# A two-layer mixture of experts in split fp32: first layers of nine units by seven block products

## The chip, the cores and the metric

The kernel runs on one core of one Trainium2 chip. TensorE (PE) does the matmuls, VectorE (DVE), ScalarE (ACT) and GpSimd (POOL) the elementwise work, SyncE (SP) issues most transfers. The metric is device microseconds of one execution; less is better. Three runs of a kernel give a median.

## The reference

```python
# attention: 2 batches x 8 heads, 576 tokens, head size 64; scores under (row maximum - tau) are masked
x = attention(q, k, v, tau)                       # -> x [1152, 512]
for e in range(4):                                # four experts, features 1024
    h = np.maximum(x @ w1[e], 0.0)
    out += p[:, e:e + 1] * (h @ w2[e])
x = out
h = np.maximum(x @ w_in, 0.0)                     # features 2048
return (h * h @ w_out).astype(np.float32)
```

## The kernel before

Every fp32 operand of the experts is split into a high part that TensorE's fast fp32 form holds exactly and a low part, and each product is three matmuls: high x high, high x low, low x high. The last two matrices (w_in, w_out) are taken as two more "experts", so that there are NE = 6, each in two halves of 512 features: twelve **units** (e, half).

A unit has a first layer (`unit_range`, L755): for each of four feature blocks f and each token range, four 128-deep steps of x with three matmuls each, into a "ph" bank. Then ACT writes the ReLU's high part (L764) and DVE its low part (L768); for the last two experts the chain is ACT ReLU (L781), DVE square (L784), ACT high (L787), POOL low (L791), through three "u" buffers. The second layer (`chunk`, L824) is nine token chunks of 128, each twelve 512-wide matmuls into one of two "m" banks, added up on DVE (L836, L840). Three units ("early") take tokens 0 to 511 while attention still runs, and tokens 512 to 1151 after it. The other nine take token ranges of 512, 320 and 320 at once: 48 matmuls of 512 and 96 of 320 in a first layer. In the text "the nine units" are these.

Weights come in groups of 128 x 1024 (`group`): SP loads one into one of two "wraw" buffers, ACT casts the high part (L685), POOL subtracts the low part (L688) into one of four "w" slots; four groups a unit. The weights of the last two experts are stored as 64-bit numbers; `convert` narrows them in 32 steps (L632 load, DVE L637, L642, L647, ACT square L652, DVE L656, L661 store). In the second layer of unit (3, 1), `turn_x` transposes the result into the x of the last two experts (L859, L864, L867).

All operations are put in an order ahead of time: `plan` schedules them by estimated times, ranks (lower goes first) and free slots, PE's own order of units being a fixed chain. Each engine then runs its list in that order, and a waiting instruction holds up what stands behind it on its engine.

Of the kernel before, what the change touches and what calls it, by code (L numbers as in the profile page):

```python
# [18 lines left out]
N = B * S  # L19
# [159 lines left out]
def attention_moe_kernel(ctx, tc, qT, kT, kD, vp, tau, probs, wa, wb, wc, wd, out):  # L179
# [16 lines left out]
        "wraw": 2, "w": 4, "ha": 1, "h": 1, "ph": 4, "wide": 1, "dbl": 2, "u": 3,  # L196
# [411 lines left out]

    def end_attention():
        attn.close()  # L610
        open_pools(ctx, "h", "wide", "dbl", "u")
        rest = ctx.enter_context(tc.tile_pool(name="acc", bufs=1))
        accs[1] = rest.tile([P, NCH - EARLY // P, DM], F32, name="acc1")
        open_pools(ctx, "ph", space=PSUM)
# [8 lines left out]
    def convert(e, w, g):  # L623
        key = e, w, g
        stores[key] = []
        for z in range(2):
            wb_, db = Buf("wide"), Buf("dbl")
# [12 lines left out]
            def second(wb_=wb_, db=db):  # L640
                o = db.tile
# [3 lines left out]
            def third(wb_=wb_, db=db):  # L645
                o = db.tile
                nc.vector.scalar_tensor_tensor(  # L647
                    o, wb_.tile[:, :, 1], -(1 << 30), o, ALU.bitwise_and, ALU.bitwise_or)
# [5 lines left out]
            def fourth(wb_=wb_, db=db):  # L654
                m, f = wb_.tile.bitcast(F32)[:, :, 1], db.tile.bitcast(F32)
                nc.vector.scalar_tensor_tensor(f, m, LEAST, f, ALU.is_ge, ALU.mult)  # L656

            def store(db=db, z=z):
                if key not in narrow:
                    narrow[key] = dram_p.tile([P, 2, 512], F32, tag=f"n{e}{w}{g}", name=f"n{e}{w}{g}")  # L660
                nc.sync.dma_start(narrow[key][:, z], db.tile.bitcast(F32))  # L661
# [34 lines left out]

    pe_last = [None]
# [23 lines left out]

    def unit(e, half, ranges, early):

        rank = 10000 + seq[0]
        gs = [group(e, 0, 2 * half + x, rank) for x in range(2)]
        gs2 = []
        for n0, widths in ranges:
            unit_range(e, half, n0, widths, early, gs, gs2, rank)

    def unit_range(e, half, n0, widths, early, gs, gs2, rank):  # L730
        n1 = n0 + sum(widths)
        firsts = [(n0 + sum(widths[:n]), w) for n, w in enumerate(widths)]

        hb = Buf("ha" if early else "h")
        width = EARLY if early else N
        h_ops = {}

        def h_tiles():
            if hb.tile is None:
                hb.tile = [new(hb, [P, FH, width], F32R, f"{hb.pool}{n}") for n in ("hi", "lo")]  # L740
            return hb.tile

        for f in range(FH):
            for t0, step in firsts:
# [14 lines left out]
                if unturned:  # L759
                    turn_x(unturned.pop())  # L760
                c0 = t0

                def relu(f=f, c0=c0, step=step, pb=pb):
                    nc.scalar.activation(h_tiles()[0][:, f, c0:c0 + step], pb.tile, AF.Relu)  # L764

                def low(f=f, c0=c0, step=step, pb=pb):
                    oh, ol = (h[:, f, c0:c0 + step] for h in h_tiles())
                    nc.vector.scalar_tensor_tensor(ol, pb.tile, 0.0, oh.bitcast(F32), ALU.max, ALU.subtract)  # L768

                r = -5000  # L770
                deps = [last] if early else [last, late]
                if e < E:
                    a = op("ACT", 0.02 + step / 1110, relu, deps, [pb, hb], r, 0.16)
                    b = op("DVE", 0.07 + step / 966, low, [a], [pb, hb], r, 0.15)
                    h_ops[f, t0] = b
                else:
                    ub = Buf("u")

                    def relu_u(ub=ub, pb=pb, step=step):
                        ub.tile = new(ub, [P, step], F32)  # L780
                        nc.scalar.activation(ub.tile, pb.tile, AF.Relu)  # L781

                    def square(ub=ub, pb=pb):
                        nc.vector.scalar_tensor_tensor(ub.tile, pb.tile, 0.0, ub.tile, ALU.max, ALU.mult)  # L784

                    def high2(ub=ub, f=f, c0=c0, step=step):
                        nc.scalar.copy(h_tiles()[0][:, f, c0:c0 + step], ub.tile)  # L787

                    def low2(ub=ub, f=f, c0=c0, step=step):
                        oh, ol = (h[:, f, c0:c0 + step] for h in h_tiles())  # L790
                        nc.gpsimd.tensor_sub(ol, ub.tile, oh.bitcast(F32))  # L791

                    a = op("ACT", 0.12 + step / 1000, relu_u, deps, [pb, ub], r)
                    b = op("DVE", 0.16 + step / 960, square, [a], [pb, ub], r)
                    c = op("ACT", 0.15 + step / 1000, high2, [b], [ub, hb], r + 1)
                    h_ops[f, t0] = op("POOL", 0.2 + 2.6 * step / 1000, low2, [c], [ub, hb], r + 1)
        if not gs2:
            gs2 += [group(e, 1, 2 * half + x, rank + 20) for x in range(2)]
        turned = []
        for n in range(n0 // P, n1 // P):  # L800
            needs = [o for (f, t0), o in h_ops.items() if t0 < (n + 1) * P and n * P < t0 + dict(firsts)[t0]]
# [3 lines left out]
            for cut in cuts:  # L805
                chunk(e, half, n, cut, needs, h_ops, hb, gs2)
            if (e, half) == (E - 1, 1):
                turned.append(n)
                if len(turned) > 1:
                    turn_x(turned[-2])  # L810
        unturned.extend(turned[-1:])

    def chunk(e, half, n, cut, needs, h_ops, hb, gs2):
        ob = Buf("m")
        width = cut.stop - cut.start
        for x in range(2):
            def mm(x=x, n=n, ob=ob):
                if x == 0:
                    ob.tile = new(ob, [P, width], F32)
                for f in (2 * x, 2 * x + 1):  # L820
                    hi, lo = (w[:, f % 2, cut] for w in gs2[x][2].tile)
                    ah, al = (h[:, f, n * P:(n + 1) * P] for h in hb.tile)
# [4 lines left out]
            need = [h_ops[k] for k in h_ops if h_ops[k] in needs and k[0] // 2 == x]  # L827
            last = pe(6 * (width / 2400 + 0.0135), mm, need + list(gs2[x][:2]), [ob, hb, gs2[x][2]])
# [24 lines left out]
    def turn_x(n):  # L853
# [7 lines left out]
        oh, ol = xhi[:, :, n * P:(n + 1) * P], xlo[:, :, n * P:(n + 1) * P]  # L861

# [5 lines left out]

        a = pe(0.45, turn, [acc_ops[n], late], [tb])
        b = op("ACT", 0.6, high, [a], [tb], -4000)  # L870
        x2[n] = op("DVE", 0.7, low, [b], [tb], -4000)

    for e, w, g in NARROWED:
        convert(e, w, g)
    for e, half, ranges, early in UNITS:
# [68 lines left out]
```

## Time and profile before

| | us |
|---|---|
| median of 3 runs (lowest, highest) | 751.4 (750.18, 752.2) |
| span of the profiled execution | 748.9 |
| first and second layer of a full unit | 25.02, 24.50 |

The page has no time of its own for the profiled execution beside its span, which runs from its first to its last instruction; the median of the runs is 2.5 us above it. Matmuls overlap, so a matmul's busy time is longer than the step from one to the next.

### The profile page before, as it was taken

The numbers are of one execution on the slowest core, as the hardware profiler recorded it, in microseconds if no ns is written. First come the engines' busy times: TensorE is split into PE (matmuls) and PEld (weight loads), VectorE is DVE, ScalarE is ACT, GpSimd is POOL, SyncE is SP. The second block draws the span as 40 slices with busy tenths as digits, with TensorE's granted clock in tenths as the row PEclk, the third lists the DMA queues.
The fourth block names the chain that finished last, engine by engine and source line by source line (L and its number), as shares of the span: only waits on it lengthen the run. The fifth ranks groups of instructions, "written<-read, shape, count | busy, mean of one in ns | idle before, by whom it ended". The sixth has DMA issues, their size and how long they took to land.

```text
span 748.9 us, 10557 instructions
## 1 busy us (share of the span) xinstructions
PE 736.9 (98%) x4118; PEld 617.9 (83%) x4118; DVE 376.0 (50%) x692; ACT 307.8 (41%) x542; POOL 325.5 (43%) x284
## 2 busy tenths in 40 slices
PE   7899999999999999999999999999999999999998
PEld 4556677887798998988989889888888898898887
DVE  6877765656256445645447454545665022222222
ACT  5887785756432232312304223123264352250430
POOL 3797879998443333112204121122066173461530
PEclk9999999999999999999999999999999999999999
DMA  6644323111223543433333424332334020100002
GB/s 228 229 145 151 104 59 124 64 56 53 80 83 114 197 145 105 158 112 104 108 112 100 141 72 140 100 112 77 105 106 134 15 84 29 57 29 28 1 29 98
DMA packets 26001, 74.70 MB, mean 100 GB/s; under 512 B 3040, under 2 KB 5472, under 8 KB 25952
## 3 DMA queue, kind: packets, MB, share of 16 engines
q1 hardware_dynamic: 24368, 71.55, 28.9%
q10 hardware_dynamic: 1584, 2.49, 0.9%
q8 instruction: 32, 0.52, 0.3%
q14 instruction: 17, 0.14, 0.1%
HBM read 63.28 MB, written 10.75 MB: 99 GB/s over the span
## 4 chain that ended last, share of the span: by engine, by line
PE 92%; POOL 3%; DVE 2%; ACT 1%; issue 1%; DMA 1%; SPq 0%; DVEq 0%; POOLq 0%; ACTq 0%
PE m L824 39%; PE ph L755 36%; PE tv L543 5%; PE m L755 4%; PE tv L487 4%; PE s L381 2%; PE s L395 2%; DVE nm L400 1%; POOL p L466 1%; DVE p L421 1%; DMA k<-in_kT_dram 1%; POOL wlo L688 1%; PE ph L859 1%; PE tv L508 0%; POOL q L274 0%
## 5 line engine op out<-in xcount | busy, mean ns | idle before, releaser
L688 POOL TENSOR_TENSOR wlo<-wraw,whi 128x1024 fp32r<-128x1024 f32 x60 | 146.9, 2460 | 321.6 <-ACT whi L685 302.0
L755 PE MATMUL ph<-xlo,whi 128*128 128x320 f32 (+1 forms) x528 | 175.0, 331 | 0.0
L755 PE MATMUL ph<-xhi,whi 128*128 128x320 f32 (+1 forms) x528 | 174.9, 331 | 0.0
L755 PE MATMUL ph<-xhi,wlo 128*128 128x320 f32 (+1 forms) x528 | 174.7, 331 | 0.0
L824 PE MATMUL m<-whi,hhi 128*128 128x512 f32 (+1 forms) x388 | 150.9, 389 | 0.0
L824 PE MATMUL m<-wlo,hhi 128*128 128x512 f32 (+1 forms) x388 | 150.2, 387 | 0.0
L824 PE MATMUL m<-whi,hlo 128*128 128x512 f32 (+1 forms) x388 | 150.2, 387 | 0.0
L755 PEld LDWEIGHTS ph<-xhi,whi 128*128 128x128 f32 x528 | 99.1, 188 | 6.4
L755 PEld LDWEIGHTS ph<-xlo,whi 128*128 128x128 f32 x528 | 99.1, 188 | 6.1
L755 PEld LDWEIGHTS ph<-xhi,wlo 128*128 128x128 f32 x528 | 99.1, 188 | 5.9
L685 ACT CAST whi<-wraw 128x1024 fp32r<-128x1024 f32 x60 | 63.2, 1053 | 97.2 <-PE m L824 86.8
L836 DVE SCALAR_TENSOR_TENSOR acc<-m,pn,acc 128x512 f32<-128x512 f32 x63 | 47.3, 750 | 86.6 <-PE m L824 86.6
L824 PEld LDWEIGHTS m<-whi,hlo 128*128 128x128 f32 x388 | 72.9, 188 | 14.9
L824 PEld LDWEIGHTS m<-whi,hhi 128*128 128x128 f32 x388 | 72.9, 188 | 14.4
L824 PEld LDWEIGHTS m<-wlo,hhi 128*128 128x128 f32 x388 | 72.9, 188 | 14.2
L764 ACT ACTIVATE hhi<-ph 128x320 fp32r<-128x320 f32 (+1 forms) x84 | 39.7, 476 | 98.0 <-PE ph L755 97.8
L466 POOL TENSOR_TENSOR p<-p,r 128x576 f32<-128x576 f32 x64 | 72.3, 1149 | 8.8 <-DVE r L448 8.1
L768 DVE SCALAR_TENSOR_TENSOR hlo<-ph,hhi 128x320 fp32r<-128x320 f32 (+1 forms) x84 | 44.7, 537 | 58.0 <-ACT hhi L764 57.8
L784 DVE SCALAR_TENSOR_TENSOR u<-ph,u 128x320 f32<-128x320 f32 (+1 forms) x48 | 26.8, 559 | 83.6 <-ACT u L781 83.5
L791 POOL TENSOR_TENSOR hlo<-u,hhi 128x320 fp32r<-128x320 f32 (+1 forms) x48 | 50.2, 1047 | 31.8 <-ACT hhi L787 30.6
L421 DVE SCALAR_TENSOR_TENSOR p<-s,th,p 128x576 f32<-128x576 f32 x59 | 47.5, 815 | 21.8 <-POOL th L405 15.5
L400 DVE TENSOR_REDUCE nm<-s 128x1 f32<-128x576 f32 x67 | 48.6, 751 | 13.5 <-PE s L381 7.5
(90 smaller groups left out, 911.1 us busy)
## 6 DMA issues: line engine op xcount, KB each, us to landing
wraw<-in_wa_dram SPq DMA_DIRECT2D x22, 512.0 KB, 4.0
wraw<-in_wb_dram SPq DMA_DIRECT2D x22, 512.0 KB, 3.5
wide<-in_wc_dram SPq DMA_DIRECT2D x16, 512.0 KB, 4.4
n<-dbl SPq DMA_DIRECT2D x32, 256.0 KB, 3.4
wide<-in_wd_dram SPq DMA_DIRECT2D x16, 512.0 KB, 3.9
wraw<-n SPq DMA_DIRECT2D x16, 512.0 KB, 3.3
v<-in_vp_dram SPq DMA_DIRECT2D x12, 320.0 KB, 3.2
k<-in_kT_dram SPq DMA_DIRECT2D x8, 432.0 KB, 4.4
```

The costliest lines, as they stand in the source:

```text
L400: nc.vector.tensor_reduce(t["nm"], sb.tile[:, :, :HW], AX.XY, ALU.max, negate=True)
L421: nc.vector.scalar_tensor_tensor(p, sb.tile[:, :, :HW], t["th"], p, ALU.is_ge, ALU.mult, accum_out=sm["sm"][:, z:z + 1])
L466: nc.gpsimd.tensor_mul(p, p, sums[i]["r"][:, y:y + 1].to_broadcast([P, S]))
L543: nc.tensor.matmul(ob.tile[z * D:(z + 1) * D, :], tiles["v"][:, vc, :], pts[g].tile[:, ch, :], start=(n == 0), stop=(n == QT),)
L685: nc.scalar.copy(sb.tile[0], rb.tile)
L688: nc.gpsimd.tensor_sub(sb.tile[1], rb.tile, sb.tile[0].bitcast(F32))
L755: nc.tensor.matmul(pb.tile, w, m, start=(c == 0 and n == 0), stop=(c == DC - 1 and n == 2))
L764: nc.scalar.activation(h_tiles()[0][:, f, c0:c0 + step], pb.tile, AF.Relu)
L768: nc.vector.scalar_tensor_tensor(ol, pb.tile, 0.0, oh.bitcast(F32), ALU.max, ALU.subtract)
L791: nc.gpsimd.tensor_sub(ol, ub.tile, oh.bitcast(F32))
L824: nc.tensor.matmul(ob.tile, w, m, start=(f == 0 and y == 0), stop=(f == FH - 1 and y == 2))
L836: nc.vector.scalar_tensor_tensor(a, ob.tile, pn[:, n, e:e + 1], a, ALU.mult, ALU.add)
```

## The change

The nine units that take all tokens at once get another first layer (`paired`). Weights, x and result are each cut into 2 x 2 blocks: model features in two halves, unit features in two halves, tokens in pairs of 64-token runs (the even runs and the odd runs of each token range). The product of the blocks is taken by seven block products instead of eight. This needs sums of blocks: S1 to S4 of the weights (`sums`, POOL, then split again by ACT and POOL into "s12" and "s34"; A22 is split apart into "a22"), and four sums of x (`th`, `tl`), made once after attention (`pair_up`) and again in `turn_x`. Tokens 0 to 511 and 512 to 1151 are the two groups g; a set is a group and one of two feature blocks, and its products have 256 or 320 columns. Products are accumulated in PSUM banks A, B, C; partial sums that are needed twice are copied by ACT into "sn" (`keep`) and added by DVE (`join`), for one result into a fourth bank D. Products 1 to 3 read x itself, every second run of 64 tokens; 4 to 7 read the sums. "ph" has five banks instead of four. `convert` keeps its unfinished words in a new "pd" bank of PSUM instead of in "dbl", which has one buffer instead of two. h lies in two buffers, "ha" and "hb". The ReLU chains move into `finish`, the second layer's loop into `outputs`, with the same operations. The scratch area for transfers is set to 1024 bytes.

```diff
@@ sets, slots and units
+GROUPS = ((0, EARLY // 2), (EARLY, (N - EARLY) // 2))
+TW = P // 2
+PIECES = ((2, 2), (3, 2))
...
-UNITS += [(e, h, [(0, (512, 320, 320))], False) for e in range(NE) for h in range(2) if (e, h) not in EARLY_UNITS]
+UNITS += [(e, h, "paired", False) for e in range(NE) for h in range(2) if (e, h) not in EARLY_UNITS]
...
-        "wraw": 2, "w": 4, "ha": 1, "h": 1, "ph": 4, "wide": 1, "dbl": 2, "u": 3,
+        "wraw": 2, "w": 4, "ha": 1, "hb": 1, "ph": 5, "wide": 1, "pd": 1, "dbl": 1, "u": 3,
+        "s12": 1, "s34": 1, "a22": 1, "swt": 1, "sn": 4, "xf": 2,
@@ convert (second and third change as first does)
-            def first(wb_=wb_, db=db):
-                db.tile = new(db, [P, 512], I32)
+            def first(wb_=wb_, pb=pb):
+                pb.tile = new(pb, [P, 512], I32)
                 nc.vector.tensor_scalar(
-                    db.tile, wb_.tile[:, :, 1], 5, 2, ALU.logical_shift_left, ALU.logical_shift_right)
+                    pb.tile, wb_.tile[:, :, 1], 5, 2, ALU.logical_shift_left, ALU.logical_shift_right)
...
+            def fourth(wb_=wb_, pb=pb, db=db):
+                db.tile = new(db, [P, 512], F32)
+                m, f = wb_.tile.bitcast(F32)[:, :, 1], pb.tile.bitcast(F32)
+                nc.vector.scalar_tensor_tensor(db.tile, m, LEAST, f, ALU.is_ge, ALU.mult)
@@ sums (new): the weights of one unit's first layer
+                if n == 1:
+                    nc.gpsimd.tensor_add(s1, a21, a22)
+                elif n == 2:
+                    nc.gpsimd.tensor_sub(s2, s1, a11)
+                elif n == 3:
+                    nc.gpsimd.tensor_sub(s3, a11, a21)
+                else:
+                    nc.gpsimd.tensor_sub(s4, a12, s2)
...
+        def high_s(z):
+            def f():
+                sbs[z].tile = [new(sbs[z], [P, 2, 2, H], F32R, f"{ROWS[z]}{n}") for n in ("hi", "lo")]
+                nc.scalar.copy(sbs[z].tile[0], tb.tile[:, 2 * z:2 * z + 2])
+            return f
+
+        def low_s(z):
+            def f():
+                nc.gpsimd.tensor_sub(sbs[z].tile[1], tb.tile[:, 2 * z:2 * z + 2], sbs[z].tile[0].bitcast(F32))
+            return f
@@ pair_up (new): th and tl from x, before the first of the nine units
+                def fetch(d=d, k=k, pb=pb, x_of=x_of, w=w):
+                    pb.tile = new(pb, [P, w], F32)
+                    nc.scalar.copy(rows_of(pb.tile), x_of(xhi, d, k).bitcast(F32))
+
+                def whole(d=d, k=k, pb=pb, out=None, x_of=x_of, part=part):
+                    o = part(out) if out else pb.tile
+                    nc.vector.tensor_add(rows_of(o), rows_of(pb.tile), x_of(xlo, d, k).bitcast(F32))
...
+            def high(fb=fb, made=made):
+                nc.scalar.copy(made(th), fb.tile[:, :4])
+
+            def low(fb=fb, made=made):
+                nc.gpsimd.tensor_sub(made(tl), fb.tile[:, :4], made(th).bitcast(F32))
@@ paired (new): one unit
+            name, blocks = {
+                1: ("A11", (0, 0)), 2: ("A12", (1, 0)), 3: ("S4", (1, 1)), 4: ("A22", (1, 0)),
+                5: ("S1", (0, 0)), 6: ("S2", (1, 1)), 7: ("S3", (0, 1)),
+            }[n]
+            bank = s["B"] if n == 2 else s["C"] if n in (3, 5) else s["A"]
...
+            own = n >= 4
+
+            def moving(z, c):
+                if own:
+                    return (th, tl)[z][g][:, (0, 2, 3, 1)[2 * d + k], c]
+                return halves_of((xhi, xlo)[z][:, 2 * d + c, n0:n0 + 2 * w])[:, :, k]
...
+                for c in range(2):
+                    for y, (a, b) in enumerate(((0, 0), (0, 1), (1, 0))):
+                        nc.tensor.matmul(
+                            bank.tile if own else rows_of(bank.tile), of(a, fp, c), moving(b, c),
+                            start=(start and c == 0 and y == 0), stop=(c == 1 and y == 2), skip_group_check=True)
...
+        def keep(s, bank, after):
...
+                nc.scalar.copy(sb.tile, bank.tile)
...
+        def join(s, out, bank, kept, after):
...
+                nc.vector.tensor_add(out.tile, bank.tile, sb.tile)
...
+        def fourth(s):
+            m4 = product(4, s, False, [s["d"]])
+            ready_h(s, s["A"], s["f"] + 2, 0, m4)
+
+        def third(s):
+            m3 = product(3, s, False, [s["k5"][0]])
+            c12 = join(s, s["C"], s["C"], s["k2"], m3)
+            ready_h(s, s["C"], s["f"], 1, c12)
+
+        def seventh(s):
+            m7 = product(7, s, False, [s["k2"][0]])
+            s["d"] = join(s, s["D"], s["A"], s["k5"], m7)
+            ready_h(s, s["D"], s["f"] + 2, 1, s["d"])
+
+        for n, s in enumerate(sets):
+            m1 = product(1, s, True, [])
+            if unturned:
+                turn_x(unturned.pop())
+            k1 = keep(s, s["A"], m1)
+            m5 = product(5, s, True, [])
+            s["k5"] = keep(s, s["C"], m5)
+            m2 = product(2, s, True, [])
+            c11 = join(s, s["B"], s["B"], k1, m2)
+            ready_h(s, s["B"], s["f"], 0, c11)
+            m6 = product(6, s, False, [k1[0]])
+            s["k2"] = keep(s, s["A"], m6)
+            if n:
+                fourth(sets[n - 1])
+            if n < len(sets) - 1:
+                third(s)
+                seventh(s)
+            else:
+                seventh(s)
+                third(s)
+                fourth(s)
@@ turn_x: the sums of the x of the last two experts
+        def sub(z):
+            def f():
+                d, k, y = ((0, 0, 4), (1, 1, 0), (1, 1, 4), (1, 0, 1))[z]
+                pair = block(d, k), part(y)
+                nc.vector.tensor_sub(part(z), *(pair if z else pair[::-1]))
+            return f
...
+        kept = op("ACT", 0.2, keep, [a], [tb, fb], -4000, 0.16)
...
+        c = op("ACT", 0.6, high_t, list(subs.values()), [fb], -3990, 0.18)
+        x_pairs.setdefault((1, g), []).extend([c, op("POOL", 1.35, low_t, [c], [fb], -3990)])
@@ the build
-    nc = _bacc.Bacc("TRN2", target_bir_lowering=False, num_devices=1)
+    nc = _bacc.Bacc("TRN2", target_bir_lowering=False, num_devices=1, dynamic_dma_scratch_size=1024)
```

## Rows read from the trace of the kernel before

**Rows 1.** The page: its span, and each engine's busy time.
```profile
span 748.9 us, 10557 instructions
...
PE 736.9 (98%) x4118; PEld 617.9 (83%) x4118; DVE 376.0 (50%) x692; ACT 307.8 (41%) x542; POOL 325.5 (43%) x284
```

**Rows 2.** Busy us by stretch: PE, PEld, DVE, ACT, POOL (x count); clock, DMA share, GB/s.
```profile
212.36:295.48 83.12, 83.12 (x469) 75.99 (x468) 46.39 (x69) 26.41 (x43) 29.43 (x12) 1.00 0.43 143
...
295.48:320.50 25.02, 25.02 (x146) 23.07 (x144) 16.86 (x22) 9.13 (x16) 7.63 (x3) 1.00 0.39 127
...
320.50:345.00 24.50, 24.50 (x110) 20.27 (x109) 11.10 (x18) 3.75 (x5) 2.40 (x1) 1.00 0.28 90
...
596.89:621.90 25.01, 25.01 (x145) 23.06 (x144) 6.21 (x11) 13.05 (x25) 17.54 (x13) 1.00 0.18 64
```

**Rows 3.** Waits of PE, whole span, the longest (us, times, longest).
```profile
PE tv L487 <- ACT pt L492: 2.8, 2, 1.9
```

**Rows 4.** PE in order of time: start us, us, instruction; 320 and 512 wide.
```profile
299.81 0.31 PE L755 MATMUL ph<-xhi,wlo 128*128 128x320 f32 x1
...
301.72 0.39 PE L755 MATMUL ph<-xhi,whi 128*128 128x512 f32 x1
...
304.46 0.30 PE L755 MATMUL ph<-xhi,whi 128*128 128x320 f32 x1
```

**Rows 5.** The same, 256 wide, first and last of 24.
```profile
742.73 0.28 PE L824 MATMUL m<-whi,hhi 128*128 128x256 f32 x1
...
745.48 0.28 PE L824 MATMUL m<-whi,hlo 128*128 128x256 f32 x1
```

**Rows 6.** Groups by line: weight loads of the first layers (busy us, mean ns).
```profile
L755 PEld LDWEIGHTS ph<-xhi,whi 128*128 128x128 f32 x528 | 99.1, 188 | 6.4
```

**Rows 7.** Groups by line and shape on ACT, DVE and POOL (busy us, mean ns).
```profile
L764 ACT ACTIVATE hahi<-m 128x256 fp32r<-128x256 f32 x8 | 3.2, 397 | 0.0
...
L685 ACT CAST whi<-wraw 128x1024 fp32r<-128x1024 f32 x60 | 63.2, 1053 | 97.2 <-PE m L824 86.8 <-issue 10.4
...
L652 ACT ACTIVATE wide<-wide 128x512 f32<-128x512 f32 x32 | 21.4, 669 | 77.0 <-DVE dbl L647 68.9 <-issue 7.4 <-ACT whi L685 0.8
...
L840 DVE TENSOR_TENSOR acc<-m,acc 128x512 f32<-128x512 f32 x26 | 18.0, 692 | 51.8 <-PE m L824 51.8
...
L840 DVE TENSOR_TENSOR acc<-m,acc 128x256 f32<-128x256 f32 x2 | 0.8, 425 | 1.8 <-PE m L824 1.8
...
L688 POOL TENSOR_TENSOR wlo<-wraw,whi 128x1024 fp32r<-128x1024 f32 x60 | 146.9, 2460 | 321.6 <-ACT whi L685 302.0 <-PE m L824 19.0
...
L791 POOL TENSOR_TENSOR hlo<-u,hhi 128x320 fp32r<-128x320 f32 x32 | 29.4, 919 | 9.0 <-ACT hhi L787 8.0
...
L791 POOL TENSOR_TENSOR hlo<-u,hhi 128x512 fp32r<-128x512 f32 x16 | 20.8, 1302 | 22.9 <-ACT hhi L787 22.6
```

**Rows 8.** DVE narrowing steps and POOL subtractions in order of time.
```profile
253.62 0.69 DVE L656 SCALAR_TENSOR_TENSOR dbl<-wide,dbl 128x512 f32<-128x512 f32 x1
...
295.50 5.22 POOL L688 TENSOR_TENSOR wlo<-wraw,whi 128x1024 fp32r<-128x1024 f32 x2 [9.59 <-ACT whi L685]
...
299.24 2.03 DVE L656 SCALAR_TENSOR_TENSOR dbl<-wide,dbl 128x512 f32<-128x512 f32 x1 [0.79 <-ACT wide L652]
```

**Rows 9.** ACT and DVE in order of time, behind PE and each other.
```profile
300.16 0.44 ACT L764 ACTIVATE hhi<-ph 128x320 fp32r<-128x320 f32 x1 [0.47 <-PE ph L755]
...
243.80 0.44 ACT L764 ACTIVATE hhi<-ph 128x320 fp32r<-128x320 f32 x1 [1.32 <-PE ph L755]
...
244.27 0.49 DVE L768 SCALAR_TENSOR_TENSOR hlo<-ph,hhi 128x320 fp32r<-128x320 f32 x1 [0.80 <-ACT hhi L764]
```

**Rows 10.** Loads to be narrowed, first and last start; the page's row of their stores.
```profile
L632 SPq DMA_DIRECT2D wide<-in_wc_dram x16: 327/350/427, 201.1 to 523.2; - x16
...
L632 SPq DMA_DIRECT2D wide<-in_wd_dram x16: 328/350/393, 254.8 to 571.2; - x16
...
n<-dbl SPq DMA_DIRECT2D x32, 256.0 KB, 3.4
```

More of the change, by code (lines that the diff above doesn't have):

```diff
@@ new lines, in finish, with part, shaped, relu @@
+    def finish(e, f, at, step, last, pb, hb, width, paired=True):
+        r = -5000
+        def part(n):
+            if hb.tile is None:
+                hb.tile = [new(hb, [P, FH, width], F32R, f"{hb.pool}{x}") for x in ("hi", "lo")]
+            t = hb.tile[n][:, f]
+            return halves_of(t)[:, :, at] if paired else t[:, at:at + step]
+        def shaped(t):
+            return rows_of(t) if paired else t
+        def relu():
+            nc.scalar.activation(part(0), shaped(pb.tile), AF.Relu)
+        def low():
+            nc.vector.scalar_tensor_tensor(
+                part(1), shaped(pb.tile), 0.0, part(0).bitcast(F32), ALU.max, ALU.subtract)
+        if e < E:
+            a = op("ACT", 0.02 + step / 1110, relu, last, [pb, hb], r, 0.16)
+            return op("DVE", 0.07 + step / 966, low, [a], [pb, hb], r, 0.15)
+        ub = Buf("u")
+        def relu_u():
+            ub.tile = new(ub, [P, step], F32)
+            nc.scalar.activation(ub.tile, pb.tile, AF.Relu)
+        def square():
+            nc.vector.scalar_tensor_tensor(ub.tile, pb.tile, 0.0, ub.tile, ALU.max, ALU.mult)
+        def high2():
+            nc.scalar.copy(part(0), shaped(ub.tile))
+        def low2():
+            nc.gpsimd.tensor_sub(part(1), shaped(ub.tile), part(0).bitcast(F32))
+        a = op("ACT", 0.12 + step / 1000, relu_u, last, [pb, ub], r)
+        b = op("DVE", 0.16 + step / 960, square, [a], [pb, ub], r)
+        c = op("ACT", 0.15 + step / 1000, high2, [b], [ub, hb], r + 1)
+        return op("POOL", 0.2 + 2.6 * step / 1000, low2, [c], [ub, hb], r + 1)
@@ L770, in unit_range @@
[L770 to L796, printed above, removed]
@@ L797, in unit_range, with needs @@
+                h_ops[f, t0] = finish(e, f, t0 - base, step, [last] if early else [last, late], pb, hb, width, False)
         if not gs2:
             gs2 += [group(e, 1, 2 * half + x, rank + 20) for x in range(2)]
-        turned = []
-        for n in range(n0 // P, n1 // P):
-            needs = [o for (f, t0), o in h_ops.items() if t0 < (n + 1) * P and n * P < t0 + dict(firsts)[t0]]
+        rows = range(n0 // P, (n0 + sum(widths)) // P)
+        def needs(n, x):
+            return [o for (f, t0), o in h_ops.items()
+                    if f // 2 == x and t0 < (n + 1) * P and n * P < t0 + dict(firsts)[t0]]
@@ L803, in unit_range, with outputs @@
+        outputs(e, half, rows, needs, lambda n: (hb, base), gs2)
+    def outputs(e, half, rows, needs, h_of, gs2):
+        for n in rows:
             end = (e, half, n) == (NE - 1, 1, NCH - 1)
@@ L825, in mm @@
                             ob.tile, w, m, start=(f == 0 and y == 0), stop=(f == FH - 1 and y == 2))
[L827 to L828 removed]
+            last = pe(6 * (width / 2400 + 0.0135), mm, needs(n, x) + list(gs2[x][:2]), [ob, hb, gs2[x][2]])
         def accumulate(ob=ob, n=n, e=e, half=half):
```

222 lines of the change are left out of this document (183 added, 39 removed).

## The prediction

> **What bounds the kernel now.** I read the page first, then the busy time by stretch, then the waits of the matmul engine, then single matmuls in order of time. The page shows TensorE (PE) busy 98% of a span of 748.9 us, twice as much as any other engine [rows 1]. [...] Of the time after 212 us no wait of PE is listed at all; its few waits all lie in attention, the largest 2.8 us [rows 3]. So from 212 us on, the kernel costs what its matmuls cost to issue, and a gain must come as fewer or shorter matmuls. A full unit is a first layer of 25.02 us and a second layer of 24.50 us [rows 2].
>
> **What a matmul costs.** A busy time of one matmul (0.31 or 0.39 us) holds a pipeline's latency, so I take start to start. Thirteen steps of 320-wide ones go from 299.81 to 301.72: 146.9 ns each. Twelve steps of 512-wide ones go from 301.72 to 304.46: 228 ns [rows 4]. The only 256-wide ones at full pace are the last 24 of the program: 23 steps from 742.73 to 745.48, 119.6 ns each [rows 5]. Check: 48 x 228.3 + 96 x 146.9 = 25.06 us, against the 25.02 us of the stretch.
>
> **The main term.** A first layer goes from 144 matmuls (48 of 512, 96 of 320) to 4 sets x 7 products x 6 = 168: 84 of 256 and 84 of 320. That is 84 x 0.1196 + 84 x 0.1469 = 22.39 us, so 2.63 us less than the 25.02. Nine units: 23.7 us. The second layers, attention and the tail are the same instructions.
>
> The weight loads grow from 144 to 168 and every matmul still has its own. Each lasts 188 ns [rows 6], longer than 119.6 ns, yet the steps of 256 are even [rows 5]: loads overlap at that pace too, so I add nothing. [...]
>
> The moving operand of products 1 to 3 is now read in runs of 64 with gaps. No matmul of the trace reads so. Lower bound 0; upper bound half pace: 3/7 of 22.39 us again, 9.6 us a unit. The nearest row is VectorE reading every second word of a tile: 0.69 us for 512 when undisturbed, the same as a dense 512 [rows 7, 8]. I take 0.
>
> **The new waits on PE's path.** Seven products need banks and copies that eight independent sums did not. Work per set [rows 7, 9]: three ACT copies and four ReLUs at 0.40 us (256; 0.44 for 320); three DVE joins and four low parts at 0.425 us, the PSUM row of 256 (0.49 for 320). ACT 2.8 to 3.1 us, DVE 3.0 to 3.4 us, in a set of 42 x 0.1196 = 5.0 or 42 x 0.1469 = 6.2 us. So they fit on average, and what counts is latency:
> - Product 7 waits for the copy of bank A taken after product 6. In the first set only product 3 lies between, 6 x 0.12 = 0.72 us. ACT begins 0.04 us after a set's last matmul ends (299.81 + 0.31, then 300.16) and DVE 0.03 us after ACT [rows 9]. From the start of product 6's last matmul: 0.28 + 0.04 + 0.40 + 0.05 = 0.77 us, against 0.84 us at which product 7 may start. It just fits if ACT is free. The last set is the same with product 4 of the set before, 0.88 us, between; its product 4 waits for the join after product 7 in the same way. In the middle sets two products lie between.
> - Each set takes four of five banks. The third new bank of a set (product 2, 1.44 us in) needs the one in which the set before ended product 3: join, ReLU, low part, about 0.43 + 0.40 + 0.42 and three hand-overs, done some 1.0 us into the set. Slack about 0.4 us.
> - Behind a copy that waits stand the ReLUs on ACT, behind a join the low parts on DVE, and those hold banks.
> What can be in front: a weight cast of 1.05 us or a square of 0.67 us on ACT, a narrowing step of 0.69 us on DVE. In a first layer some three casts and two squares, 4.5 us of 22.4, make ACT foreign-busy 20% of the time. Two tight places a set, four sets, 20%, some 0.3 us beyond the slack: 0.5 us a unit. Bounds: 0 (the trace of before, with its own planned order, shows 0), and 1.05 + 0.69 less 0.5 of slack in each set, 5 us a unit. I take 0.5 us, nearer the lower end, as the busy shares leave much room [rows 2]: 9 x 0.5 = 4.5 us.
>
> Narrowing in a PSUM bank makes DVE's blocking steps shorter: the same step took 0.69 us with POOL idle and 2.03 us with POOL in a weight subtraction [rows 8]. [...] The joins, the sums of x and the narrowing all keep one operand in PSUM, so I expect no 2 us steps; it costs or saves PE nothing by itself.
>
> **Work that is added under cover.** Sums of x: eight pieces, each four ACT copies, eight DVE steps, a cast and a POOL subtraction; at most 27 us on DVE (0.425 each), 21 on ACT, 20 on POOL, in the 83 us between attention and the first of the nine units, where they are busy 46, 26 and 29 us [rows 2]. They share one "pd" bank with the narrowing: 32 passes of some 1.2 us and eight narrowings of 4.5 us, 75 of 83 us. Cost 0; if the last piece is late, set 2 of the first unit waits once, a few us.
> Weights: POOL gains four sums and one low part of 512 (1.30 us each by the 512 row) and one low part of 1024 (2.46): 9 us a unit, five casts on ACT instead of four. For the first five units POOL has 19 of 46.9 us of work. The S tiles have one buffer and are rewritten in the 24.5 us of the second layer: 2 x 2.46 + 1.30 = 6.2 us. The loads of the second layer's weights come after them, on SP's queue, and land (4 us) with half a stretch to spare. Cost 0.
> In the unit that turns x, DVE gets about 0.69 + 0.69 + 4 x 0.4 = 3.0 us per chunk of 3.1 us, and two banks of second-layer sums wait for it; the first-layer need for the last chunks comes ten us later. I take 0 to 2 us, within the 4.5. The one-slot "dbl" costs nothing: a narrowing takes some 12 us and its store 3.4 [rows 10].
>
> **Sum.** 748.9 - 23.7 + 4.5 = 729.7 us of span. The runs' median of 751.4 us lies 2.5 us above the span shown, so 732.2 us.
>
> **Rivals.**
> 1. POOL falls behind in the last four units, where each h needs a POOL subtraction (0.92 us for 320, about 0.75 for 256): 16 of them are 13.3 us, and weights for the next unit up to 9.9 us more, 23.2 in 22.4 us. With three "u" buffers ACT then stops before a ReLU with the copies behind it. For it: that stretch already shows 17.5 of 25.0 us. Against: half the weight work can go into the second layer. Price: 0.8 us and one 2.46 us subtraction, 3.3 us x 4 = 13 us: 745 us.
> 2. Slower: the bank chain. If each set's product 2 finds its bank late, that alone decides; the point is 2.63 us a unit, 0.66 us a set on top of the slack of 0.4. Against: one ACT cast in front of the ReLU in every set would be needed. With a cast (1.05) and a narrowing step (0.69) in front each time, 1.34 us a set are lost, 5.4 us a unit: 751.4 + 9 x (5.4 - 2.63) = 776 us; halfway 755 us.
> 3. PE doesn't keep its pace, by gapped reads at half pace or by loads of 188 ns that hold the matmul: 9 x 9.6 = 86 us more, about 814 us (loads: 168 x 0.188 = 31.6 us a unit, 811 us). The steps speak against the loads [rows 4 to 6], and against the gaps nothing but the DVE row [rows 8].
> 4. No stall at all: 751.4 - 23.7 = 727.7 us, the floor.
>
> **Chances.** My forecast with stalls of 0 to 1.4 us a unit (727.7 to 740 us): 0.74. Rival 1 or a like loss, 740 to 749 us: 0.11. Stalls that just cancel the gain: 0.04. Rival 2: 0.08. Rival 3: 0.03. What this kernel's measurement can tell from no change is about 0.3%, 2.3 us. Faster 0.85, same 0.04, slower 0.11. Range: 727 (the floor with 0.7 us of run to run) to 745 us, which leaves out 0.15 above that and half of rival 1's band. The likeliest case alone: 728 to 740.
>
> **What would show it.** First-layer stretches of 22.4 to 23.4 us, nine of them, and second layers still 24.5 us. Steps of 120 and 147 ns inside a product, gapped or not. PE waits that begin with product 7 or 2 and name ACT copies or DVE low parts. DVE narrowing steps all near 0.7 us. I am wrong if PE waits above 1.4 us a unit are listed, if a 256-wide step of products 1 to 3 is longer than those of 4 to 7, or if the last four units lose more than the first five by over 2 us each.

## The result and the profile after

The changed kernel takes 731.27 us (median of 4 runs, 730.22 to 731.71), the kernel before 751.79 us beside it (750.18 to 752.2): a ratio of 0.9731, interval 0.9716 to 0.9746. Forecast were 732.2 us, 727 to 745. The profiled executions differ by 748.9 - 729.1 = 19.8 us of span.

The page of the kernel after, its span and busy times, against [rows 1]:

```profile
span 729.1 us, 11749 instructions
...
PE 716.8 (98%) x4334; PEld 613.1 (84%) x4334; DVE 427.7 (59%) x936; ACT 379.1 (52%) x778; POOL 423.0 (58%) x371
```

PE is still busy 98% of the span, which is shorter: the time went where it bounds. The other three engines went up by 9 to 15 points and still have room.

Busy time by stretch, against [rows 2] (start:end and length; then busy us of PE, PEld, DVE, ACT and POOL with counts, PE's granted clock, DMA share, GB/s): the time from attention to the first of the nine units, then the first and second layer of that unit, the first layers of the second and the fifth, the turning of x, and the first layers of the sixth, unit (4,0), and of the eighth.

```profile
212.87:295.97 83.10, 83.10 (x470) 76.01 (x468) 59.81 (x132) 40.63 (x84) 50.05 (x27) 1.00 0.45 144
295.97:318.46 22.49, 22.49 (x169) 22.45 (x168) 15.60 (x34) 13.77 (x32) 12.87 (x8) 1.00 0.45 137
318.46:342.97 24.51, 24.51 (x111) 20.28 (x109) 12.69 (x20) 4.85 (x8) 6.62 (x5) 1.00 0.44 139
342.97:365.74 22.77, 22.63 (x169) 22.43 (x168) 16.13 (x35) 14.37 (x32) 13.10 (x8) 1.00 0.37 117
...
484.49:507.22 22.73, 22.70 (x169) 22.44 (x168) 16.56 (x35) 14.17 (x31) 13.17 (x8) 1.00 0.36 118
507.22:535.43 28.21, 28.21 (x142) 23.30 (x141) 22.18 (x55) 13.32 (x29) 13.28 (x10) 1.00 0.29 94
535.43:559.95 24.52, 23.74 (x176) 23.08 (x174) 18.35 (x45) 19.62 (x51) 22.41 (x21) 1.00 0.25 74
...
584.45:607.01 22.56, 22.56 (x169) 22.45 (x168) 11.11 (x26) 16.74 (x43) 19.77 (x18) 1.00 0.14 48
```

The nine first layers take 22.49, 22.77, 22.44, 22.78, 22.73, 24.52, 22.56, 22.55 and 22.53 us. Their sum is 205.37 us, before 225.72 (25.59 in unit (4,0), which holds a transpose, and 25.0 in the others): 20.35 us less. The second layers (24.5 us) and the turning of x (28.21) are as long as before, and the first unit starts 0.5 us later. 20.35 - 0.5 is the difference of the spans.

All waits of PE behind 205 us (total us, times, longest) are one row:

```profile
PE ph L966 <- DVE u L917: 0.8, 2, 0.5
```

This view lists idle time between the modelled end of a matmul and the start of the next, so a step that is only a little late can be missing from it. Product 5 of the second set in the second unit is 0.30 us late (a step of 0.42 us instead of 0.12) and isn't in that row:

```profile
347.87 0.28 PE L966 MATMUL ph<-xhi,wlo 128*128 128x256 f32 x1
348.29 0.39 PE L966 MATMUL ph<-th,s12hi 128*128 128x256 f32 x1
```

PE and ACT in order of time, in the first set of the first unit (start us, us, instruction): the end of product 3, the beginning of product 7, and the copy of bank A for which product 7 waits.

```profile
299.08 0.28 PE L966 MATMUL ph<-xhi,s34lo 128*128 128x256 f32 x1
299.20 0.28 PE L966 MATMUL ph<-xhi,s34hi 128*128 128x256 f32 x1
299.32 0.28 PE L966 MATMUL ph<-xlo,s34hi 128*128 128x256 f32 x1
299.44 0.28 PE L966 MATMUL ph<-xhi,s34lo 128*128 128x256 f32 x1
299.56 0.39 PE L966 MATMUL ph<-th,s34hi 128*128 128x256 f32 x1
299.78 0.28 PE L966 MATMUL ph<-tl,s34hi 128*128 128x256 f32 x1
299.90 0.28 PE L966 MATMUL ph<-th,s34lo 128*128 128x256 f32 x1
...
299.14 0.37 ACT L981 COPY sn<-ph 128x256 f32<-128x256 f32 x1
```

Product 3 reads xhi and xlo in runs of 64 with gaps, product 7 reads the dense th and tl; both step by 0.12 us. By the same rows the copy ends at 299.51 and product 7 starts at 299.56, on its beat. Only the step behind it is 0.22 us instead of 0.12.

Two of the four narrowing steps and the joins, of the groups by line and shape on DVE (count; busy us, mean ns; idle us before them and what ended it):

```profile
L652 DVE SCALAR_TENSOR_TENSOR pd<-wide,pd 128x512 int32<-128x512 int32 x32 | 22.1, 690 | 0.5
L667 DVE SCALAR_TENSOR_TENSOR dbl<-wide,pd 128x512 f32<-128x512 f32 x32 | 21.9, 684 | 6.3 <-ACT wide L662 5.3
...
L991 DVE TENSOR_TENSOR ph<-ph,sn 128x256 f32<-128x256 f32 x54 | 23.2, 430 | 39.1 <-PE ph L966 35.3 <-ACT hahi L920 2.5 <-ACT sn L981 0.6
```

All four narrowing steps have means of 684 to 690 ns, and none is near the 2 us of [rows 8]. The joins cost the forecast 0.43 us.

### The profile page after: what moved, and what is told of

Read it like the earlier page. It is cut to its first block, busy times and chain, and to the rows that moved or that the text cites. A ratio compares the mean times of both kernels' runs of the same rounds, so it can differ in the third digit from the quotient of the medians.

```text
span 729.1 us, 11749 instructions
## 1 busy us (share of the span) xinstructions
PE 716.8 (98%) x4334; PEld 613.1 (84%) x4334; DVE 427.7 (59%) x936; ACT 379.1 (52%) x778; POOL 423.0 (58%) x371
## 4 chain that ended last, share of the span: by engine, by line
PE 92%; POOL 3%; DVE 2%; ACT 2%; issue 1%; POOLq 0%; DVEq 0%; ACTq 0%
PE m L1104 40%; PE ph L966 27%; PE ph L1066 6%; PE tv L548 5%; PE tv L492 4%; PE m L1066 4%; PE s L386 3%; PE s L400 2%; POOL wlo L699 1%; POOL p L471 1%; PE tv L585 1%; DVE nm L405 1%; ACT pt L497 0%; PE tv L513 0%; DVE p L426 0%
## 5 line engine op out<-in xcount | busy, mean ns | idle before, releaser
L699 POOL TENSOR_TENSOR wlo<-wraw,whi 128x1024 fp32r<-128x1024 f32 x42 | 100.6, 2401 | 180.1 <-ACT whi L696 166.9
L1104 PE MATMUL m<-whi,hbhi 128*128 128x512 f32 (+1 forms) x244 | 94.6, 388 | 0.0
L1104 PE MATMUL m<-whi,hblo 128*128 128x512 f32 (+1 forms) x244 | 94.1, 386 | 0.0
L1104 PE MATMUL m<-wlo,hbhi 128*128 128x512 f32 (+1 forms) x244 | 94.1, 386 | 0.0
L991 DVE TENSOR_TENSOR ph<-ph,sn 128x256 f32<-128x256 f32 (+1 forms) x108 | 50.1, 464 | 59.2 <-PE ph L966 54.6
L1115 DVE SCALAR_TENSOR_TENSOR acc<-m,pn,acc 128x512 f32<-128x512 f32 x63 | 47.2, 750 | 60.2 <-PE m L1104 60.0
L1104 PE MATMUL m<-whi,hahi 128*128 128x512 f32 x192 | 76.5, 398 | 0.0
L1104 PE MATMUL m<-whi,halo 128*128 128x512 f32 x192 | 74.9, 390 | 0.0
L1104 PE MATMUL m<-wlo,hahi 128*128 128x512 f32 x192 | 74.9, 390 | 0.0
L1104 PEld LDWEIGHTS m<-whi,hblo 128*128 128x128 f32 x244 | 45.8, 188 | 9.4
L1104 PEld LDWEIGHTS m<-wlo,hbhi 128*128 128x128 f32 x244 | 45.9, 188 | 9.0
L1104 PEld LDWEIGHTS m<-whi,hbhi 128*128 128x128 f32 x244 | 45.8, 188 | 8.9
L966 PE MATMUL ph<-xhi,whi 128*128 128x256 f32 (+1 forms) x144 | 43.0, 298 | 0.8 <-DVE u L917 0.8
L966 PE MATMUL ph<-th,s12hi 128*128 128x256 f32 (+1 forms) x144 | 42.9, 298 | 0.2
```

Of the source, the lines that this page charges most:

```text
L699: nc.gpsimd.tensor_sub(sb.tile[1], rb.tile, sb.tile[0].bitcast(F32))
L966: nc.tensor.matmul(bank.tile if own else rows_of(bank.tile), of(a, fp, c), moving(b, c), start=(start and c == 0 and y == 0), stop=(c == 1 ...
L991: nc.vector.tensor_add(out.tile, bank.tile, sb.tile)
L1104: nc.tensor.matmul(ob.tile, w, m, start=(f == 0 and y == 0), stop=(f == FH - 1 and y == 2))
L1115: nc.vector.scalar_tensor_tensor(a, ob.tile, pn[:, n, e:e + 1], a, ALU.mult, ALU.add)
```

## The experiments

Where not said otherwise, the lengths of first layers are in the order of the units and each kernel is compared with the changed one by the medians. Ratios are to the kernel before.

**Five units of nine.** The four units of experts 4 and 5 go back to plain sums, with their late ranges split in two, and the sums of x for them are left out.

```diff
-UNITS += [(e, h, "paired", False) for e in range(NE) for h in range(2) if (e, h) not in EARLY_UNITS]
+UNITS += [(e, h, "paired", False) for e in range(E) for h in range(2) if (e, h) not in EARLY_UNITS]
+UNITS += [(e, h, [(0, (512,)), (EARLY, (320, 320))], False) for e in range(E, NE) for h in range(2)]
...
```

> Only the five units of the first four experts keep the seven products; the four units of the last two experts have plain first layers again (512 and 2 x 320 columns), and the turning of x makes no sums. Theory A (the gain is PE's issue time, unit by unit, and the added work lies under cover): the five units of the changed kernel took 22.44 to 22.78 us, mean 22.64, against 25.02, so 5 x 2.38 = 11.9 us remain of the gain: 739.9 us, ratio 0.984; the last four first layers at 25.0 us (25.6 in the one with a transpose). Rival (the sums of x and the POOL work of the last two experts cost time elsewhere too, so that those four units bring less than their first layers show): 737 us or below.

745.27 us (745.07 to 745.29), ratio 0.9917 [0.9902, 0.9931]; 5.4 us above the 739.9. The five paired first layers are as in the changed kernel (22.51, 22.80, 22.47, 22.78, 22.67 us). The excess lies in my variant: its second layer is cut in two, and its short first part waits for POOL (`PE m L1107 <- POOL halo L924: 2.5, 4, 0.6`). By the steps that part is some 1.3 us longer in each of the four units than 48 steps of 0.228 us. So this run did not answer the question, and it was put again.

**Five units, first layers whole.** As above, but a plain unit finishes both halves of its first layer before its second layer, as in the kernel before.

```diff
         for n0, widths in ranges:
-            unit_range(e, half, n0, widths, early, gs, gs2, rank)
+            unit_range(e, half, n0, widths, early, gs, gs2, rank, both if len(ranges) > 1 and not early else None)
+        if both:
+            outputs(e, half, range(NCH), lambda n, x: both[int(n >= EARLY // P)][0](n, x),
                    lambda n: both[int(n >= EARLY // P)][1], gs2)
...
```

> As the first experiment with five units of seven products, but the four plain units make their whole first layer ahead of their second layer, as in the kernel before (the split one had PE wait for POOL's low parts, 0.8 us and smaller steps in each unit). Theory A (unit by unit): 751.3 - 11.9 = 739.4 us, the last four first layers 25.0 to 25.6 us. Rival (the first five units' gain is partly lost elsewhere): 742 us or more.

739.70 us (739.19 to 740.19), ratio 0.9849 [0.9832, 0.9865]: as expected. First layers 22.50, 22.80, 22.45, 22.79 and 22.66, then 25.55, 24.95, 24.95 and 24.95; no wait of PE is listed behind 205 us. The last four units are worth 739.70 - 731.27 = 8.4 us. By stretches it is 25.55 - 24.52 and 3 x 2.4, 8.2 us, and the first unit starts 0.2 us later. The gain adds up unit by unit.

**Four banks.** One bank less for the sums of a set.

```diff
-        "wraw": 2, "w": 4, "ha": 1, "hb": 1, "ph": 5, "wide": 1, "pd": 1, "dbl": 1, "u": 3,
+        "wraw": 2, "w": 4, "ha": 1, "hb": 1, "ph": 4, "wide": 1, "pd": 1, "dbl": 1, "u": 3,
```

> The ph pool has four banks as in the kernel before, all else as changed. Theory A (the banks handed from set to set have some tenths of a us of slack with five and none with four): product 5 (0.72 us into a set) waits for the bank of product 3 of the set before (free at about 1.0 us), product 2 for the bank of the join after product 7 (free at about 1.7 us, wanted at 1.44): 0.3 to 0.6 us at each of 27 passages from set to set, 8 to 16 us: 739 to 747 us, PE waits naming DVE low parts or squares. Rival (the fifth bank only smooths; PE pace alone sets the time): 731 to 732 us.

750.52 us (749.7 to 751.73), ratio 0.9987 [0.9978, 0.9996]: 19 us more, nearly the whole gain. With one bank less the planner also put the work of ACT, DVE and POOL in another order, so the 19 us belong to the bank together with that order. First layers 25.51, 25.87, 24.33, 24.30, 24.14, 28.71, 24.36, 24.39, 23.70. The longest waits of PE behind 205 us:

```profile
PE ph L966 <- DVE halo L904: 3.4, 5, 1.3
PE ph L966 <- DVE u L917: 2.8, 11, 0.4
PE ph L966 <- ACT xg L1162: 2.0, 1, 2.0
```

The change of sets at 406.6 us in order of time, PE and DVE:

```profile
406.34 0.31 PE L966 MATMUL ph<-xhi,wlo 128*128 128x320 f32 x1
406.61 0.41 PE L966 MATMUL ph<-th,s12hi 128*128 128x320 f32 x1
...
406.14 0.97 DVE L904 SCALAR_TENSOR_TENSOR halo<-ph,hahi 128x256 fp32r<-128x256 f32 x2
```

Product 5, the second of a set, now finds its bank still held by a low part of the set before: a step of 0.27 us instead of 0.147 here, and single waits of up to 2.0 us elsewhere. Over the nine units the late starts of product 5 and those of product 2 add up to some 8 us each. The mechanism is that of rival 2, at product 5 as well as at product 2, and it is dearer than I expected. Five banks keep most of it out. Some 1.4 us of the 19 came by PE's clock: behind the wait of 2.0 us in unit (4,0) the granted clock is 0.50 from 550.24 to 553.65, and a 256-wide step takes 0.21 us there instead of 0.12.

**The copy twice.** Each copy of a bank into "sn" is issued twice, so that everything behind it is some 0.4 us later.

```diff
                 nc.scalar.copy(sb.tile, bank.tile)
+                nc.scalar.copy(sb.tile, bank.tile)
```

> Each of the three copies of a set that ACT makes for later joins is made twice, in the same order of all else: 0.29 us (256) or 0.35 us (320) more on ACT, 108 times. Theory A (product 7 of a unit's first set, and products 7 and 4 of its last, wait with no slack for such a copy, the others have some): 0.3 us in the first and 0.3 us in the last set, 0.6 us a unit: 736 to 737 us. Rival 1 (ACT is half idle, all is absorbed): 731.5 us. Rival 2 (all twelve copies of a unit are on the path): 12 x 0.32 us a unit, 34 us: 765 us.

740.63 us (739.6 to 741.77), ratio 0.9861 [0.9844, 0.9877]: 9.4 us more, 1.0 us a unit. First layers 23.31, 24.08, 23.32, 23.95, 23.74, 26.31, 23.67, 23.39, 23.39. PE's wait (total, times, longest) and the first set of the first unit in order of time:

```profile
PE ph L966 <- ACT sn L982: 4.4, 16, 0.6
```

```profile
298.36 0.28 PE L966 MATMUL ph<-xhi,s34lo 128*128 128x256 f32 x1
298.45 0.37 ACT L982 COPY sn<-ph 128x256 f32<-128x256 f32 x1
...
298.88 0.39 PE L966 MATMUL ph<-th,s34hi 128*128 128x256 f32 x1 [0.24 <-ACT sn L982]
299.10 0.28 PE L966 MATMUL ph<-tl,s34hi 128*128 128x256 f32 x1
```

The stalls sit at product 7 of the first set (here 0.52 us instead of 0.12) and of the last, two places that the prediction called tight. These late starts, with the late step behind each, make 7.8 of the 9.8 us by which the nine first layers are longer; 1.3 us more stand at product 3 of the first set, in three units. Each late product also has a next step of 0.22 us. The places were right and the size too small: I had counted the late start alone.

**Two "u" buffers.** Rival 1 rested on how far POOL may fall behind before ACT stops.

```diff
-        "wraw": 2, "w": 4, "ha": 1, "hb": 1, "ph": 5, "wide": 1, "pd": 1, "dbl": 1, "u": 3,
+        "wraw": 2, "w": 4, "ha": 1, "hb": 1, "ph": 5, "wide": 1, "pd": 1, "dbl": 1, "u": 2,
```

> Two u buffers instead of three for the h of the last two experts, all else as changed. With three, no wait of PE or ACT names POOL. Theory A (POOL keeps up; what counts is how many h of a set are under way at once: three products end within 1.5 us and each holds a u for some 2.7 us): with two, ACT stops before a ReLU with the copies behind it, 0.5 to 1 us in each of 16 sets, 8 to 16 us, in the last four units alone: 739 to 747 us. Rival (POOL or the u buffers have room to spare): 731.5 us.

734.88 us (733.83 to 735.54), ratio 0.9782 [0.9766, 0.9797]: 3.6 us more, between the two expectations. The first five first layers are unchanged; the last four take 25.84, 23.24, 24.07 and 22.55 us, with `PE ph L966 <- DVE u L917: 3.2, 5, 1.4`. ACT's ReLUs now wait for POOL's low parts (`ACT u L914 <- POOL hblo L923: 4.8, 7, 1.3`), which they did once, for 0.5 us, in the changed kernel; the expectation has it that they never did. So the third buffer keeps POOL's delay away from ACT and PE there. With the other order of ACT's, DVE's and POOL's work that goes with it, it is worth 3.6 us.

**The next set earlier.** In the first set, product 1 of the next set goes ahead of product 7, to give the copy another 0.7 us.

```diff
                 third(s)
+                if not n:
+                    begin(sets[1])
                 seventh(s)
...
```

> In the first set of a unit, product 1 of the next set goes ahead of product 7, so that product 7 has two products and not one between it and the copy it waits for; all else as changed. Theory A (that copy comes about 0.1 us late in each of nine units): 1 to 1.5 us less, 730 us, and no longer step at the start of product 7 in the first sets. Rival (the bank that product 1 takes early is missed later): no gain, waits move to products 5 and 2 of the second set.

731.42 us (729.86 to 731.49), ratio 0.9732 [0.9717, 0.9746]: not to be told from the changed kernel. The late step at product 7 of the first sets went, and the first layers sum to 204.86 us, 0.5 less. But unit (4,0) took 0.6 us longer (a wait on the DVE square of 1.3 us). So the late step at product 7, some 0.1 us a unit, was worth no time that the runs can show.

**Narrowing in place in SBUF.** The words lie in the one "dbl" buffer that is also stored from, not in a bank.

```diff
-            wb_, pb, db = Buf("wide"), Buf("pd"), Buf("dbl")
+            wb_, db = Buf("wide"), Buf("dbl")
+            pb = db
...
-                nc.vector.scalar_tensor_tensor(db.tile, m, LEAST, f, ALU.is_ge, ALU.mult)
+                nc.vector.scalar_tensor_tensor(f, m, LEAST, f, ALU.is_ge, ALU.mult)
```

> The narrowing keeps its words in the SBUF buffer again (one buffer, written in place), all else as changed. Theory A (DVE steps of 2 us beside POOL come back, but the joins have slack): narrowing steps with two SBUF inputs up to 2.0 us beside POOL; first five units 0.1 to 0.5 us longer each, last four the same: 731.5 to 734 us. Rival (the narrowing in PSUM is what makes the change pay): a blocked step costs PE over 1 us, about one a set: 740 us or more.

760.65 us (759.93 to 764.68), ratio 1.0133 [1.0105, 1.0161]: 29 us more, slower than the kernel before. The rival was right. The profiled execution is the slowest of the four (764.68). In it first layers take up to 27.9 us; PE waits for copies (9.0 us in 3 times), for accumulations (8.0) and for squares (3.7). The four steps have means of 1023, 1237, 1290 and 952 ns. Four times behind a wait of PE of 1.4 to 3.0 us the granted clock falls to 0.50, for instance from 408.48 to 411.89; by the longer steps this costs some 5.9 us. DVE also waited 7.7 us for the stores of the one buffer, and the planned order was another. So two more runs.

**The same with two buffers.** As above, and besides:

```diff
-        "wraw": 2, "w": 4, "ha": 1, "hb": 1, "ph": 5, "wide": 1, "pd": 1, "dbl": 1, "u": 3,
+        "wraw": 2, "w": 4, "ha": 1, "hb": 1, "ph": 5, "wide": 1, "pd": 1, "dbl": 2, "u": 3,
...
```

> The narrowing in SBUF as in the experiment that measured 760.65 us, but with two dbl buffers, as in the kernel before (one buffer had made DVE wait 7.7 us for stores). Theory P (DVE steps with two SBUF operands are held up by POOL, 1.2 us instead of 0.69 on average and up to 2.7, and joins stand behind them): most of the loss stays, 745 to 760 us, PE waits naming copies, joins and accumulations in the first five units. Theory S (it was the store of the single buffer): 731 to 735 us.

736.29 us (735.04 to 738.98), ratio 0.9806 [0.9783, 0.983]: 5 us more, between the two expectations. Steps of 799, 1070, 955 and 980 ns. The order of the work was again another. To make room, the two kinds of buffer for the sums of x share their space here and in the next run.

**The same order.** Every engine keeps the order of the changed kernel; only the narrowing's words lie in an SBUF tile "nar" of their own in place of the bank.

```diff
-                pb.tile = new(pb, [P, 512], I32)
+                pb.tile = pools["nar"].tile([P, 512], I32, tag="nar", name=f"nar{e}{w}{g}{z}")
...
```

> Every engine's order is that of the changed kernel; only the tile in which the narrowing keeps its words lies in SBUF instead of the pd bank (the sums of x still pass through pd; the two kinds of buffer for sums of x share their space to make room). Theory P (two SBUF operands make DVE wait for POOL, whatever the order): narrowing steps of 1 us on average instead of 0.69, PE waits in the first five units that name ACT copies, joins or low parts, 735 to 745 us. Theory O (the order that goes with the buffers made the losses of the two SBUF variants, 760.65 and 736.29 us): 731 to 733 us.

746.37 us (746.25 to 747.49), ratio 0.9944 [0.993, 0.9957]: 15 us more, a little above the range of theory P. Two steps, of its groups on DVE by line and shape, and the first of them by itself (ns: shortest/median/longest):

```profile
L652 DVE SCALAR_TENSOR_TENSOR nar<-wide,nar 128x512 int32<-128x512 int32 x32 | 37.4, 1170 | 0.5
L647 DVE TENSOR_SCALAR nar<-wide 128x512 int32<-128x512 int32 x32 | 29.1, 911 | 4.8 <-DMA wide<-in_wd_dram 2.7 <-DMA wide<-in_wc_dram 2.1
...
L647 DVE TENSOR_SCALAR nar<-wide x32: 416/452/2672, 213.2 to 576.8; 128x512 int32<-128x512 int32 x32
```

The first layer of the fifth unit in order of time, POOL, DVE and PE, with the narrowing in SBUF:

```profile
490.73 2.41 POOL L699 TENSOR_TENSOR wlo<-wraw,whi 128x1024 fp32r<-128x1024 f32 x1 [18.86 <-ACT whi L696]
...
491.63 1.79 DVE L647 TENSOR_SCALAR nar<-wide 128x512 int32<-128x512 int32 x1
493.10 2.58 POOL L728 TENSOR_TENSOR wlo<-wraw,whi 128x1024 fp32r<-128x1024 f32 x1
493.46 2.77 DVE L652 SCALAR_TENSOR_TENSOR nar<-wide,nar 128x512 int32<-128x512 int32 x1
...
495.67 0.28 PE L966 MATMUL ph<-xhi,wlo 128*128 128x256 f32 x1
497.88 0.39 PE L966 MATMUL ph<-th,s12hi 128*128 128x256 f32 x1 [1.94 <-DVE halo L904]
...
496.15 0.42 DVE L991 TENSOR_TENSOR ph<-ph,sn 128x256 f32<-128x256 f32 x1
```

And the same instructions in the changed kernel:

```profile
484.46 2.42 POOL L699 TENSOR_TENSOR wlo<-wraw,whi 128x1024 fp32r<-128x1024 f32 x1 [19.29 <-ACT whi L696]
...
485.35 0.69 DVE L647 TENSOR_SCALAR pd<-wide 128x512 int32<-128x512 int32 x1
486.07 0.69 DVE L652 SCALAR_TENSOR_TENSOR pd<-wide,pd 128x512 int32<-128x512 int32 x1
486.82 2.42 POOL L728 TENSOR_TENSOR wlo<-wraw,whi 128x1024 fp32r<-128x1024 f32 x1
486.91 0.43 DVE L991 TENSOR_TENSOR ph<-ph,sn 128x256 f32<-128x256 f32 x1
```

With the words in SBUF these steps end only when POOL's subtraction has ended (493.42 behind 493.14, 496.23 behind 495.68). That holds for the whole run: of its 128 narrowing steps 53 last over 0.8 us, and each of these ends 0.28 us (L647) or 0.55 us (the others) behind the end of an instruction of POOL. In the changed kernel 70 of the 128 lie beside POOL's work, and none lasts over 0.70 us. The join stands behind the second step: it begins 2.69 us after that step's start instead of 0.84. The low part that frees the bank comes later in turn, and PE stands idle for 1.94 us at product 5.

Not all of the 15 us are lost at joins. The second layer ahead of the first unit takes 2.8 us longer and one of the nine second layers 1.3 us, where mostly DVE's accumulations come late (`PE m L1104 <- DVE acc L1115: 2.3, 3, 1.0`). The nine first layers are 12.4 us longer, 4.8 of them in the fifth unit and 4.3 in unit (4,0). Of that some 3 us came by PE's clock. Behind the two longest waits, 1.94 and 2.12 us, the granted clock is 0.50 from 499.09 to 502.50 and from 550.29 to 553.70, and the 256-wide step there is 0.21 us instead of 0.12:

```profile
500.05 0.41 PE L966 MATMUL ph<-xhi,whi 128*128 128x256 f32 x1
500.26 0.41 PE L966 MATMUL ph<-xlo,whi 128*128 128x256 f32 x1
```

In the changed kernel the granted clock is 1.00 in every stretch behind attention.

## Why the prediction held, and where it did not

**The main term: shown.** Forecast 22.39 us a first layer, measured 22.44 to 22.78 in eight of nine units. The steps are 0.12 and 0.147 us, gapped or not, so the reads in runs of 64 cost the 0 that I chose; the half pace of my upper bound was an assumption, and no run shows it. The added weight loads are hidden too: each lasts 186 to 193 ns, PEld is busy 22.45 of 22.49 us, and the matmuls still step at 120 ns. Rival 3 falls with these steps.

**The stalls: the places were right, the size partly by luck.** 23.7 - 20.35 = 3.3 us against 4.5 forecast. About half of it, 24.52 - 22.39 less a transpose of some 0.6 us (25.59 - 25.0 before), 1.5 us, is in unit (4,0), where the squares that free "u" and the bank stand on DVE among the sums of the turned x and behind a narrowing step. For the turning I gave 0 to 2 us, but in the second layer ahead of that unit. In the other eight units it is 0.05 to 0.39 us, where the bound ran to 5. By the steps over 0.12 and 0.147 us, 2.2 us of the loss lie where a product begins a new bank (products 1, 2 and 5), and 0.9 us at product 7 or the product 4 behind it. The forecast of 0.5 us a unit came from a guess that foreign ACT work stands in the way 20% of the time. The steps don't show that share: the last three units repeat the same loss at product 7, 0.14 to 0.16 us, in a fixed order. So that part of the 4.5 us came near by luck. The copy issued twice shows that product 7 is a tight place.

**Bank slack: too kindly sized.** I gave the chain of low parts some 0.4 us of slack with five banks, and rival 2 a chance of 0.08. Not every set has that slack: with five banks a product that begins a bank is still 0.19 to 0.30 us late in three of the first five units (starts at 348.29, 447.75 and 490.42), besides the 0.8 us listed for unit (4,0). With four banks 19 us are lost. The experiment's forecast was 16 at most. (The "halfway 755 us" of that rival is 752 by its own terms, 751.4 + 9 x (2.7 - 2.63).)

**Rival 1: near, but not there.** POOL is busy 19.77 of 22.56 us in a late first layer and 22.41 of 24.52 us in unit (4,0), as I feared (23.2 of 22.4). PE waits for none of it, ACT once for 0.5 us.

**The sums of x: hidden, with more room than the forecast 8 us.** The last POOL subtraction that they need ends at 294.74, before the first unit starts at 295.97. It is a piece of the second token group (it comes behind the pieces of 768 columns, which only that group has), and PE first reads that group's sums in the third set, 11.6 us later. The rows of PE show that place; they also show the 320-wide step, 0.147 us, first with gaps and then dense.

```profile
293.44 1.30 POOL L881 TENSOR_TENSOR tl<-xf,th 128x512 fp32r<-128x512 f32 x1
...
306.01 0.31 PE L966 MATMUL ph<-xlo,whi 128*128 128x320 f32 x1
306.15 0.31 PE L966 MATMUL ph<-xhi,wlo 128*128 128x320 f32 x1
306.30 0.31 PE L966 MATMUL ph<-th,s12hi 128*128 128x320 f32 x1
306.45 0.31 PE L966 MATMUL ph<-tl,s12hi 128*128 128x320 f32 x1
```

**The sentence that failed: the narrowing in a PSUM bank "costs or saves PE nothing by itself".** I had counted DVE's share of time, and by shares DVE has room either way (62% of the span with the words in SBUF). What counts is that a step which waits for POOL is up to 2 us longer (2.77 us at 493.46 instead of 0.69) at the moment when a join, a low part or an accumulation stands behind it, at places where PE has next to no slack (348.29 above). In the same order this is worth 746.37 - 731.27 = 15 us of the 20. I also priced each wait at its own length, and the clock was no term of mine: behind the longest waits it took some 3 of the 15 us. The forecast time was right since I had taken the short steps as given, and with them no wait was long. I treated that part as an extra when it is what lets the seven products pay. That the bank would keep the steps short was my expectation: the row of 2.03 us in [rows 8] has all its operands in SBUF. The changed kernel shows it: with the words in the bank the steps stay at 0.69 us, also the 70 beside POOL's work. L647, with one SBUF input and an SBUF output, took 0.42 us at its shortest and up to 2.67 us where POOL held it.

**Open.** Three placements in SBUF lost 5, 15 and 29 us. The store waits of the single buffer (7.7 us on DVE), the half clock and other orders go into these differences; the runs don't separate them in full. The worth of the fifth bank and of the third "u" buffer is known only together with the order that the planner makes for each. No version run here was measurably faster than the changed kernel.

## What to carry to other kernels

When PE is busy all the time, price a change by steps from start to start (0.12 us here for a 256-wide matmul that is listed as busy for 0.28 us), and then look for the places in each round where a result of PE comes back to PE: each has a slack that a row or two gives, and here it came with the number of banks (19 us between four and five, with the order of work that goes with each). Read late steps from the rows of PE and not from the list of waits alone. On an engine that stands in such a return path, the longest single instruction ahead counts, not its busy share (a step of 2.77 us in SBUF ahead of a join left PE idle for 1.94 us); try DVE's filler work with its words in PSUM where POOL is subtracting at the same time (here 0.69 us a step in the bank, 2.77 us in SBUF at 493.46). Undo the parts of a change that seem to be mere housekeeping as well, in the same order of work, before calling them free.

## What the runs showed of the hardware

- Product 7 of the first set in the changed kernel, which began just as the copy it waits for had ended (299.51), started on its beat, but its second matmul came 0.22 us later instead of 0.12 (299.56 to 299.78). Behind a wait that was really late the same 0.10 us came on top (298.88 to 299.10 with the doubled copies); in that run this is so at product 7 of nearly every first and last set, and it is part of why a unit lost 1.0 us instead of 0.6.
- A DVE step with a single SBUF input and an SBUF output was held by POOL too (L647, 0.42 us at its shortest and 2.67 at its longest; 0.69 with its output in the bank). A held step ended 0.28 us (L647) or 0.55 us (two SBUF inputs) behind POOL's instruction. POOL's own subtraction went from 2.43 us at most to 2.86 at most in that run (L728).
- A moving operand read in runs of 64 with gaps cost nothing that shows at 0.12 and 0.147 us a step in the changed kernel (299.08 to 299.56, 306.01 to 306.30).
- A long wait of PE cost more than its length in three runs: the granted clock fell to 0.50 behind waits of 1.4 to 3.0 us, and a 256-wide step took 0.21 us instead of 0.12 there, some 1.5 us each time. Behind a wait of 1.4 us in the run with two "u" buffers the steps stayed at 0.12 and 0.147 us (from 549.83).
